# Five stream transposes in place of eight for the probabilities of the strided attention pieces

## The chip, the core and the metric

The kernel runs on one core of a Trainium2 chip. Its engines work side by side and wait for one another on semaphores: PE (TensorE, matrix products), DVE (VectorE), ACT (ScalarE), POOL (GpSimd) and SP (SyncE, which here only issues transfers). The metric is the device time of one launch in microseconds (us), as the median of three runs.

## The reference

Eight batches of eight heads, 576 positions of 64 features each. The first four heads see the last 32 positions, the last four heads ("strided") every 32nd position before their own. A gated layer of 512 to 1536 to 512 features follows.

```
mask_local = (rel >= 0) & (rel < 32)
mask_strided = (rel >= 0) & (pos[None, :] % 32 == pos[:, None] % 32)
scores = where(masks, 0.125 * q @ k.T, -1e9);  attn = softmax(scores)
x = (attn @ v) as 4608 x 512
out = (sigmoid(x @ w_gate) * (x @ w_val)) @ w_out
```

## The kernel before

Attention is done in pieces of two heads, four pieces to a batch, two local (even numbers) and two strided (odd numbers): 32 pieces in all. The pieces of batches 0 and 1 have names that begin with f, those of batches 2 to 7 are numbered 0 to 23. The four of batch 0 turn their probabilities on PE, and the change does not touch them. Of the 28 others, which turn theirs on DVE, 14 are strided.

Of one such piece the steps are: S, scores on PE (line 422); M, the mask added on DVE (L446); A and U, row maximum and subtraction on DVE (L462, L471); E, exponent on ACT (L486); N and W, row sum and scaling on DVE (L492, L502, L510); B, the turn on DVE; X, the weighing of the values on PE (L598 strided, L570 local), which reads the turned tile `pt`; H and R, the results copied away by ACT. Z, on POOL, sets the columns beyond the 54 keys (L380, L382), since a strided piece has 54 keys in rows of 64.

The turn of a strided piece (`turn_blocks`) has to transpose, within each half of the 128 partitions, a block of 64 x 64: queries lie on partitions, keys on columns, twelve such blocks one after another. A stream transpose turns squares of 32 x 32, so each of four bands of 32 partitions (`part`, 0 to 3) is turned in two instructions, one for each half of the columns, and each lands in its place in `pt`: eight instructions, `32x384`. For local pieces POOL first clears parts of `pt` (`clear`, step Y, L373), and eight other transposes (L534) follow. `pt`, `sb` (the probabilities) and `mx` have one buffer each.

The rest of the kernel is the gated layer. Batches 0 to 2 go through it straight: g and v (gate and value products, L677), o (L708). From batch 3 on pairs of batches go through a fast scheme with seven products in place of eight: sums of weights are built and stored (pa L892, pb L897, ph L902, pw L906, pd), groups of them loaded (r), half products G and V on PE (L980, tiles p and d), evictions c on ACT (L1002), ad, mu and sigmoids on DVE and ACT (L1007, L1024), differences ta to td (L1030), operands hx on ACT and hy on DVE or hyp on POOL (L1044, L1048), and output products Oa and Ob (L1059).

Every engine takes its instructions in the order of one list written out in the source, `ORDER`. A name that ends in p or v is the same step on the other of POOL and DVE (pa on POOL, pav on DVE). Pieces 1 to 23 of the list are spread between the products, so that PE has products while DVE works on a piece.

Of the kernel before, what the change touches and what calls it, by code (L numbers as in the profile page):

```python
# [96 lines left out]
x0.2 y0.2 wdp3.2 wu3.2 wl3.2 wlp2.2 wa4.2 o0.1 fg3.0 wd4.1 fg3.1 fQ1.2 wb4.2 s0.3 fg4.0 wdp5.0 wu5.0 ws4.2 wr7.1 m0.3 wu4.1 wl4.1 wl5.0 wb6.0 wb5.1
x0.3 y0.3 o0.2 wdp4.2 wu4.2 wa5.1 ws5.1 wd5.1 wu5.1 s0.4 fM1.1 wa6.0 wr5.2 wr6.1 wlp5.1 wa6.1 wb5.2 ws6.0 fg4.1 wlp4.2 wd6.0 wa5.2 wu6.0 wlp6.0 wr7.0
wb7.0 ws6.1 wr8.0 m0.4 wb6.1 x0.4 wd6.1 fg5.0 o0.3 wu6.1 ws5.2 wd5.2 wa7.0 pl2 ws7.0 fg5.1 wu5.2 wb6.2 wlp6.1 wa7.1 s0.5 fg6.0 wd7.0 ws7.1 wb7.1 wl5.2
wb8.0 wr8.1 wd7.1 wu7.1 wlp7.1 y0.4 m0.5 wu7.0 wl7.0 wa6.2 ws6.2 wd6.2 x0.5 y0.5 fg6.1 fA1.1 wr7.2 wa8.0 ws8.0 wb8.1 s0.6 wd8.0 wa8.1 m0.6 fg7.0 wr9.0  # L100
wb7.2 wu6.2 wl6.2 wa7.2 fU1.1 x0.6 wu8.0 ws7.2 wd7.2 ws8.1 fg7.1 s0.7 wl8.0 fg8.0 wu7.2 wl7.2 y0.6 wd8.1 o0.4 o0.5 m0.7 fE1.1 wr8.2 wa8.2 wb8.2 wr9.1
wa9.0 wb9.0 wr9.2 ws8.2 fN1.1 o0.6 ws9.0 x0.7 wd9.0 fWp1.1 fB1.1.2 fB1.1.3 wu8.1 fB1.1.1 wb9.1 wdp8.2 wu8.2 wlp8.1 fB1.1.0 wlp8.2 wa9.1 wr10.0 ws9.1
wd9.1 fg8.1 wb9.2 wu9.0 wl9.0 wa9.2 ws9.2 y0.7 wu9.1 s0.8 fS1.2 wa10.0 m0.8 wb10.0 wr10.1 wlp9.1 fM1.2 wdp9.2 x0.8 fg9.0 wa10.1 wu9.2 ws10.0 wdp10.0
wb10.1 wu10.0 s0.9 fV1.1 fX1.1 fA1.2 fU1.2 fE1.2 ws10.1 wd10.1 wlp9.2 wr10.2 wa10.2 fg9.1 wlp10.0 y0.8 wb10.2 ws10.2 fH1.1 wr11.0 wu10.1 fV1.2 wdp10.2
fn1.2 fN1.2 fQ1.3 fR1.1 fW1.2 fY1.2 wb11.0 o0.7 fL1.1 wa11.0 ws11.0 fg10.0 m0.9 s0.10 fS1.3 fB1.2.0 fB1.2.3 fB1.2.1 fB1.2.2 x0.9 wlp10.1 fg10.1 wr11.2
wdp11.0 wu11.0 o0.8 y0.9 wr11.1 fZ1.3 fM1.3 fA1.3 fX1.2 o0.9 fU1.3 wb11.1 wu10.2 wlp11.0 fg11.0 wlp10.2 wa11.1 ws11.1 fE1.3 wdp11.1 fH1.2 fR1.2 wu11.1
wlp11.1 m0.10 fg11.1 fN1.3 fW1.3 fV1.3 fL1.2 fB1.3.3 fB1.3.2 fB1.3.0 fB1.3.1 fX1.3 x0.10 wa11.2 ws11.2 s0.11 y0.10 m0.11 o0.10 fH1.3 fL1.3 fR1.3 g1.0
v1.0 x0.11 y0.11 wb11.2 wd11.2 wu11.2 wl11.2 oh0.11.0 s1.0 m1.0 LQ0 S0.0 M0.0 pl0 M0.1 LQ1 A0 D0 oh0.11.1 g1.1 x1.0 y1.0 U0 E0 po5 e0.0 e0.1 d0.1 Y0
# [1116 lines left out]
```

## Time and profile before

| | |
|---|---|
| median of three runs | 912.22 us (911.18 to 912.96) |
| profiled execution | 911.91 us |
| its span, first to last instruction | 910.1 us |
| PE, DVE, ACT, POOL busy | 894.6, 663.4, 470.5, 324.0 us |
| granted TensorE clock | 1.000 of full speed, all through |

The span is 1.8 us shorter than the execution's own time, which takes in what lies around it. Busy times of PE count pipelined products that overlap a little, so a wait of PE costs somewhat more than the idle time shown. The order of the instructions says where a step stands in an engine's queue; how long anything takes or waits is read from the trace.

### The profile page before, as it was taken

The numbers are of one execution on the slowest core, as the hardware profiler recorded it, in microseconds if no ns is written. First come the engines' busy times: TensorE is split into PE (matmuls) and PEld (weight loads), VectorE is DVE, ScalarE is ACT, GpSimd is POOL, SyncE is SP. The second block draws the span as 40 slices with busy tenths as digits, with TensorE's granted clock in tenths as the row PEclk, the third lists the DMA queues.
The fourth block names the chain that finished last, engine by engine and source line by source line (L and its number), as shares of the span: only waits on it lengthen the run. The fifth ranks groups of instructions, "written<-read, shape, count | busy, mean of one in ns | idle before, by whom it ended". The sixth has DMA issues, their size and how long they took to land.

```text
span 910.1 us, 17932 instructions
## 1 busy us (share of the span) xinstructions
PE 894.6 (98%) x7050; PEld 727.7 (80%) x7050; DVE 663.4 (73%) x1075; ACT 470.5 (52%) x864; POOL 324.0 (36%) x370
## 2 busy tenths in 40 slices
...
GB/s 347 328 251 136 205 116 195 207 259 242 131 207 117 154 97 226 273 268 291 256 243 252 219 240 245 215 172 206 236 169 226 185 219 197 206 200 208 219 217 131
DMA packets 116868, 193.62 MB, mean 213 GB/s; under 512 B 7600, under 2 KB 58800, under 8 KB 116784
## 3 DMA queue, kind: packets, MB, share of 16 engines
...
## 4 chain that ended last, share of the span: by engine, by line
PE 75%; DVE 17%; issue 3%; DMA 2%; ACT 2%; POOL 1%; SPq 0%; DVEq 0%; ACTq 0%
PE oc L1059 18%; PE p L980 16%; PE d L980 12%; PE o L708 8%; PE v L677 8%; PE g L677 8%; DVE pt L534 2%; DVE pt L544 2%; DVE mx L492 1%; DVE mx L462 1%; DVE sb L510 1%; DVE sb L471 1%; DVE hid L1007 1%; PE s L422 1%; DMA ring<-sets 1%
## 5 line engine op out<-in xcount | busy, mean ns | idle before, releaser
L980 PE MATMUL p<-xs,ring 128*128 128x512 f32 x864 | 209.9, 391 | 1.6 <-DVE hid L1021 0.8
L980 PEld LDWEIGHTS p<-xs,ring 128*128 128x128 f32 x864 | 161.2, 188 | 36.0 <-DVE hid L1021 0.9
L980 PE MATMUL d<-xs,ring 128*128 128x512 f32 x648 | 158.9, 390 | 0.4 <-DVE hid L1007 0.2
L980 PEld LDWEIGHTS d<-xs,ring 128*128 128x128 f32 x648 | 121.2, 188 | 26.5 <-DVE hid L1007 0.6
L1059 PE MATMUL oc<-hh,ring 128*128 128x512 f32 x312 | 104.5, 390 | 0.0
L708 PE MATMUL o<-w,hh 128*128 128x512 f32 x288 | 91.0, 397 | 0.0
L677 PE MATMUL v<-xh,w 128*128 128x512 f32 x256 | 85.3, 391 | 0.0
L677 PE MATMUL g<-xh,w 128*128 128x512 f32 x256 | 85.0, 391 | 0.2 <-ACT xh L634 0.2
L1007 DVE TENSOR_TENSOR e<-e,d 128x512 f32<-128x512 f32 x54 | 36.9, 683 | 64.9 <-PE d L980 47.0
L1059 PE MATMUL oc<-ops,ring 128*128 128x512 f32 x288 | 72.9, 389 | 0.0
L1044 ACT CAST hh<-hid 128x512 fp32r<-128x512 f32 x78 | 47.4, 621 | 47.6 <-PE oc L1059 35.7
L1030 POOL TENSOR_TENSOR hid<-hid,hid 128x512 f32<-128x512 f32 x19 | 27.8, 1466 | 115.7 <-DVE hid L1024 105.6
L1002 ACT COPY e<-p 128x512 f32<-128x512 f32 x54 | 31.7, 587 | 71.2 <-PE p L980 67.6
L1059 PEld LDWEIGHTS oc<-hh,ring 128*128 128x128 f32 x312 | 58.6, 188 | 12.1
L544 DVE STREAM_TRANSPOSE pt<-sb 32x384 f32<-32x384 f32 x112 | 63.8, 569 | 2.0
L1007 DVE TENSOR_TENSOR hid<-hid,d 128x512 f32<-128x512 f32 x54 | 36.8, 682 | 37.8 <-PE d L980 23.3
L1059 PEld LDWEIGHTS oc<-ops,ring 128*128 128x128 f32 x288 | 54.0, 188 | 11.3
L708 PEld LDWEIGHTS o<-w,hh 128*128 128x128 f32 x288 | 52.7, 188 | 11.4
L1059 PE MATMUL oc<-hl,ring 128*128 128x512 f32 x156 | 60.8, 390 | 0.1
L897 POOL TENSOR_TENSOR sum<-sum 128x128 f32<-128x128 f32 x96 | 52.0, 542 | 24.4 <-DVE sum L892 15.6
L1002 ACT COPY hid<-p 128x512 f32<-128x512 f32 x54 | 31.7, 586 | 49.3 <-PE p L980 49.1
L534 DVE STREAM_TRANSPOSE pt<-sb 32x320 f32<-32x320 f32 (+1 forms) x112 | 55.4, 494 | 2.4
...
## 6 DMA issues: line engine op xcount, KB each, us to landing
ring<-sets SPq DMA_DIRECT2D x126, 512.0 KB, 4.9
...
```

The lines of the kernel that those rows point to most:

```text
L422: nc.tensor.matmul(sc[j % len(sc)][g * m : (g + 1) * m, j // len(sc) * BANK + (s - lo) * kk : j // len(sc) * BANK + (s - lo + 1) * kk], q[ ...
L534: nc.vector.transpose(dst[band * LB : (band + 1) * LB, at : at + n, col * LB : (col + 1) * LB], src[part * LB : (part + 1) * LB, x : x + n ...
L544: nc.vector.transpose(dst[to : to + LB, :, col : col + LB], src[part * LB : (part + 1) * LB, :, h * LB : (h + 1) * LB])
L677: nc.tensor.matmul(o, w, x, start=first and n == 0, stop=last and n == len(todo) - 1)
L708: nc.tensor.matmul(acc[k][i], h[:, i * P : (i + 1) * P], w, start=f == 0 and n == 0, stop=f == NF - 1 and n == 2,)
L897: by.tensor_tensor(u[:, to], u[:, x], u[:, y], op=op)
L980: nc.tensor.matmul(to, w[:, (wi * 2 + c) * P : (wi * 2 + c + 1) * P], x[xi][:, c], start=p in (1, 2, 5) and c == j == 0, stop=c == 1 and j ...
L1002: nc.scalar.copy(x, two[m, 0])
L1007: nc.vector.tensor_tensor(x, x, two[m, 1], op=ALU.add)
L1030: by.tensor_tensor(h[to], h[x], h[y], op=ALU.subtract)
L1044: nc.scalar.copy(ops[q, p][0], hidden_tile(k, q, KEPT[str(p)]))
L1059: nc.tensor.matmul(chains[m, at], w[:, (wi * 2 + m) * P : (wi * 2 + m + 1) * P], x[xi], start=p in (1, 2, 5) and q == j == 0, stop=q == PA ...
```

## The change

`turn_blocks` now does the right halves of the columns of all 128 partitions in one instruction (part 0). Two of the four squares that this writes are in their place; two are not, and parts 1 and 2 write the lower left squares over them. Part 3 turns the two upper left squares. The square that is left out (queries 0 to 31, keys 32 to 53) is masked, since a query sees no later key; its place in `pt`, the left columns of the lower bands, is set to zero by POOL with the rest of the left columns before (`clear`, step Y, which strided pieces now have as well).

```diff
         def clear():
             pt = tiles["pt"] = pt_tile(f"pt{b}_{step}")
+            if not local:
+                nc.gpsimd.memset(pt[:, : 2 * ns * QB].rearrange("p (t k) -> p t k", k=QB)[:, :, :LB], 0.0)
+                return
             for n in (0, 2):
...
-            if "pt" not in tiles:
-                tiles["pt"] = attn_tile("pt", f"pt{b}_{step}")
             src, dst = (x[:, : 2 * ns * QB].rearrange("p (t k) -> p t k", k=QB) for x in (tiles["sb"], tiles["pt"]))
-            for h in range(2):
-                to, col = (part // 2 * 2 + h) * LB, part % 2 * LB
-                nc.vector.transpose(dst[to : to + LB, :, col : col + LB], src[part * LB : (part + 1) * LB, :, h * LB : (h + 1) * LB])
+            if part == 0:
+                nc.vector.transpose(dst[:, :, LB:], src[:, :, LB:])
+                return
+            for frm, to, col in (((1, 0, 1),), ((3, 2, 1),), ((0, 0, 0), (2, 2, 0)))[part - 1]:
+                nc.vector.transpose(
+                    dst[to * LB : (to + 1) * LB, :, col * LB : (col + 1) * LB], src[frm * LB : (frm + 1) * LB, :, :LB]
+                )
```

`ORDER` is written anew from its 187th step on. The steps are the same but for 14 clears (Y of the odd pieces, fY1.1, fY1.3) and some 80 steps that go from POOL to DVE or from DVE to POOL. One line of the list, with the weighing of piece 17:

```diff
-G3.4.1 c3.4.0.1 B17.2 pd4.2.0 r27 V3.4.1 c3.4.1.1 G3.4.2 G3.4.6 sg3.3.3 mu3.3.3 V3.4.6 V3.4.2 ad3.4.0.2 S18.1 pa5.2.0 R16 B17.0 B17.1 B17.3 X17.1
...
+S18.1 B17.2 B17.1 B17.3 pa5.2.0 R16 r27 G3.4.5 c3.4.1.6 ta3.3 ad3.4.1.2 H16 V3.4.5 M18.0 M18.1 A18 U18 E18 pb5.2.0 G3.4.7 r29 mu3.3.7 r30 mu3.4.2
+tc3.3 X17.1 Y18 LV18 N18 W18 c3.4.0.7 ad3.4.0.7 V3.4.7 c3.4.1.7 ad3.4.1.7 ph5.2.0.0 B18.0 LQ19 D18 G3.4.4 sg3.4.4 V3.4.4 r32 r31 B18.2 B18.1 B18.3 Z19
```

On DVE, at piece 15 (tiles `sb_3`, `pt_3`; `e`, `hid`, `d` and `p` are the gated layer's), the queue was before:

```order
L492 TENSOR_REDUCE mx_3_5062<-sb_3_5061 128x12
L502 RECIPROCAL mx_3_5062<-mx_3_5062 128x12
L510 TENSOR_TENSOR sb_3_5061<-sb_3_5061,mx_3_5062 128x12x54
L1007 TENSOR_TENSOR e_2_7_5153<-e_2_7_5153,d_2_4997 128x512
L544 STREAM_TRANSPOSE pt_3_5181<-sb_3_5061 32x12x32 x2
L1007 TENSOR_TENSOR hid_6_5115<-hid_6_5115,d_2_4972 128x512
L544 STREAM_TRANSPOSE pt_3_5181<-sb_3_5061 32x12x32 x6
```

and of the same piece on DVE it is now (line numbers are up to five higher):

```order
L495 TENSOR_REDUCE mx_3_5093<-sb_3_5092 128x12
L505 RECIPROCAL mx_3_5093<-mx_3_5093 128x12
L1012 TENSOR_TENSOR e_2_7_5124<-e_2_7_5124,d_2_4975 128x512
L513 TENSOR_TENSOR sb_3_5092<-sb_3_5092,mx_3_5093 128x12x54
L1012 TENSOR_TENSOR hid_6_5012<-hid_6_5012,d_2_4966 128x512
L1029 TENSOR_TENSOR hid_5_4973<-hid_5_4973,e_2_1_4964 128x512
L544 STREAM_TRANSPOSE pt_3_5148<-sb_3_5092 128x12x32
L547 STREAM_TRANSPOSE pt_3_5148<-sb_3_5092 32x12x32 x4
```

Eight transposes with an addition among them have become one of 128 partitions and four of 32, all behind the additions.

On POOL, from the padding of piece 15 on (`sum` and `sumh` are sums of weights), the queue was before:

```order
L380 MEMSET sb_3_5061 128x12
L382 MEMSET sb_3_5061 128x12x9
L906 TENSOR_TENSOR sum_2_0_4990<-sum_2_0_4990,sumh_2_0_5111 128x512
L897 TENSOR_TENSOR sum_2_1_5124<-sum_2_1_5124 128x128 x4
L1030 TENSOR_TENSOR hid_4_4901<-hid_3_4785,hid_2_4710 128x512
L906 TENSOR_TENSOR sum_2_1_5124<-sum_2_1_5124,sumh_2_1_5172 128x512
L1030 TENSOR_TENSOR hid_2_4710<-hid_4_4901 128x512
```

and on POOL it is now:

```order
L383 MEMSET sb_3_5092 128x12
L385 MEMSET sb_3_5092 128x12x9
L1035 TENSOR_TENSOR hid_4_4855<-hid_3_4751,hid_2_4713 128x512
L373 MEMSET pt_3_5148 128x12x32
L902 TENSOR_TENSOR sum_2_1_5106<-sum_2_1_5106 128x128 x4
L911 TENSOR_TENSOR sum_2_1_5106<-sum_2_1_5106,sumh_2_1_5206 128x512
L1035 TENSOR_TENSOR hid_3_4751<-hid_4_4855,hid_3_4751 128x512
```

The new clear of `pt_3` stands behind one subtraction of the gated layer and ahead of the sums of weights.

## Rows read from the trace of the kernel before

**Rows 1.** The page: span; busy us (share) and instructions of an engine.
```profile
span 910.1 us, 17932 instructions
...
PE 894.6 (98%) x7050; PEld 727.7 (80%) x7050; DVE 663.4 (73%) x1075; ACT 470.5 (52%) x864; POOL 324.0 (36%) x370
```

**Rows 2.** Stretches: length, PE, PEld, DVE, ACT, POOL busy; clock, DMA.
```profile
84.00:380.00 296.00, 292.76 (x2751) 238.23 (x2750) 242.16 (x437) 154.67 (x276) 121.84 (x168) 1.00 0.58 182
380.00:480.00 100.00, 95.91 (x1077) 77.20 (x1076) 94.95 (x156) 57.73 (x110) 53.85 (x75) 1.00 0.82 268
480.00:911.00 431.00, 426.13 (x2303) 350.57 (x2302) 258.12 (x370) 194.07 (x352) 111.27 (x87) 1.00 0.64 208
```

**Rows 3.** PE's waits, 84 to 380 us: releaser, us in total, times, longest.
```profile
PE x L598 <- PE v L677: 0.9, 1, 0.9
PE x_a L570 <- DVE pt L534: 0.7, 1, 0.7
PE s_v L422 <- DVE e L690: 0.5, 1, 0.5
```

**Rows 4.** PE's waits, 380 to 480 us, the five longest.
```profile
PE x L570 <- DVE pt L534: 1.1, 1, 1.1
PE x L598 <- DVE pt L544: 0.8, 2, 0.4
PE p L980 <- DVE hid L1021: 0.8, 1, 0.8
PE p L980 <- ACT e L1002: 0.5, 1, 0.5
PE p L980 <- ACT hid L1002: 0.3, 1, 0.3
```

**Rows 5.** PE in order of time: start, us, instructions, idle before.
```profile
118.61 0.99 PE L570 MATMUL x<-pt,vv 64*64 64x96 f32 x40
...
415.64 1.64 PE L570 MATMUL x<-pt,vv 64*64 64x96 f32 x40 [1.06 <-DVE pt L534]
```

**Rows 6.** DVE by shape: busy us, mean ns, idle before.
```profile
L544 DVE STREAM_TRANSPOSE pt<-sb 32x384 f32<-32x384 f32 x112 | 63.8, 569 | 2.0
L534 DVE STREAM_TRANSPOSE pt<-sb 32x320 f32<-32x320 f32 x84 | 42.2, 503 | 1.6
...
L446 DVE TENSOR_TENSOR sb<-s,cst 128x324 f32<-128x324 f32 x16 | 7.2, 488 | 0.0
```

**Rows 7.** POOL by shape: the clears and the padding.
```profile
L373 POOL MEMSET pt<- 128x320 f32 x28 | 9.3, 365 | 29.8 <-DVE hid L1030 20.8 <-DVE hl L701 5.2 <-PE x_a L598 3.7
L382 POOL MEMSET sb<- 128x108 f32 x16 | 3.2, 200 | 0.0
L380 POOL MEMSET sb<- 128x12 f32 x16 | 1.9, 119 | 66.0 <-DVE pt L534 66.0
```

**Rows 8.** The sums of weights by shape, on DVE and on POOL.
```profile
L897 DVE TENSOR_TENSOR sum<-sum 128x128 f32<-128x128 f32 x48 | 15.6, 326 | 1.4
L892 DVE TENSOR_TENSOR sum<-w 128x256 f32<-128x256 f32 x28 | 10.9, 434 | 3.7 <-DMA sets<-sum 3.7
...
L897 POOL TENSOR_TENSOR sum<-sum 128x128 f32<-128x128 f32 x96 | 52.0, 542 | 24.4 <-DVE sum L892 15.6 <-issue 1.5 <-POOL sb L382 0.6
L892 POOL TENSOR_TENSOR sum<-w 128x256 f32<-128x256 f32 x40 | 33.0, 843 | 51.9 <-DMA sets<-sum 22.3 <-DVE hl L701 15.9 <-DMA osets<-sum 11.9
```

**Rows 9.** DVE and POOL in order of time, near 408 and 436 us.
```profile
408.70 1.31 DVE L501 TENSOR_SCALAR mx<-mx 128x10 f32<-128x10 f32 x1
...
436.70 0.41 DVE L501 TENSOR_SCALAR mx<-mx 128x10 f32<-128x10 f32 x1
...
408.69 1.29 POOL L906 TENSOR_TENSOR sum<-sum,sumh 128x512 fp32r<-128x512 f32 x1
```

More of the change, by code (lines that the diff above doesn't have):

```diff
@@ L97 @@
[L97 to L108, printed above, removed]
@@ new lines @@
+wr10.1 wa10.1 wb10.1 s0.9 fX1.1 wu10.0 fA1.2 fU1.2 wlp9.2 fE1.2 ws10.1 wd10.1 wr10.2 wa10.2 fV1.2 fg9.1 wb10.2 y0.8 wlp10.0 ws10.2 wdp10.2 wr11.0
+wu10.1 fn1.2 fQ1.3 fN1.2 fW1.2 fH1.1 fR1.1 fg10.0 m0.9 o0.7 wa11.0 fL1.1 wb11.0 s0.10 fS1.3 wr11.1 ws11.0 fY1.2 fB1.2.0 fB1.2.3 wlp10.1 fg10.1 fB1.2.1
+fB1.2.2 wr11.2 wdp11.0 o0.8 x0.9 wu11.0 wlp11.0 wu10.2 fZ1.3 fM1.3 fA1.3 fU1.3 wb11.1 fX1.2 y0.9 m0.10 wa11.1 o0.9 fV1.3 fg11.0 fE1.3 wlp10.2 ws11.1
+wdp11.1 fH1.2 wu11.1 wlp11.1 fg11.1 fN1.3 fW1.3 fR1.2 fL1.2 fY1.3 fB1.3.0 fB1.3.1 s0.11 x0.10 fB1.3.2 fB1.3.3 wb11.2 y0.10 wa11.2 fX1.3 LQ0 o0.10
@@ new lines @@
+LV7 X7.0 ph5.0.0.1 pw5.0.0 pwp4.1.1 pd4.1.1 S8.0 LQ9 xl3.0.1 M8.0 M8.1 A8 U8 D8 oh2.3.1 pa5.0.1 pb5.0.1 Y8 pd5.0.0 E8 N8 W8 B8.2 o2.4 g2.6 R7 s2.6
+B8.0 pa5.1.0 pb5.1.0 B8.1 ph5.0.1.1 pwp5.0.1 v2.6 oh2.5.0 H7 B8.3 LV8 X8.0 Y9 m2.6 x2.6 S9.0 Z9 M9.0 M9.1 D9 oh2.5.1 g2.7 v2.7 ph5.1.0.0 pwp5.1.0 H8
+A9 U9 y2.6 E9 N9 W9 s2.7 g2.8 pd5.0.1 pa5.1.1 m2.7 pb5.1.1 pd5.1.0 xdv3.0.0 ph5.1.1.1 xh3.0.5 LQ10 LV9 xlp3.0.5 v2.8 B9.0 B9.1 B9.2 B9.3 pw5.1.1
+pd5.1.1 x2.7 y2.7 oh2.6.0 s2.8 m2.8 R8 X9.0 Y10 S10.0 M10.0 LQ11 M10.1 A10 U10 D10 oh2.6.1 H9 xd3.0.1 xdv3.0.2 xh3.0.6 v2.9 r1 LV10 E10 xh3.0.7
@@ new lines @@
+xl3.0.6 N10 x2.8 y2.8 W10 B10.0 B10.2 g2.9 B10.1 R9 xd3.0.3 o2.7 xh3.0.4 xlp3.0.4 xh3.1.2 xlp3.1.2 s2.9 B10.3 Z11 m2.9 x2.9 y2.9 oh2.8.0 X10.0 R10
+xh3.1.1 H10 xlp3.0.7 S11.0 M11.0 M11.1 D11 oh2.8.1 A11 U11 E11 N11 W11 xd3.1.0 xh3.1.5 Y11 xlp3.1.5 g2.10 s2.10 LQ12 B11.0 B11.2 r2 v2.10 m2.10 x2.10
+g2.11 y2.10 xl3.1.1 v2.11 oh2.9.0 po0 B11.1 B11.3 s2.11 m2.11 xh3.0.3 LV11 X11.0 pav0.2.0 pbv0.2.0 S12.0 M12.0 r4 H11 xd3.1.1 xh3.1.3 x2.11 M12.1 r3
+xh3.1.6 r0 A12 xlp3.1.6 y2.11 U12 LV12 xdv3.1.2 xh3.1.7 oh2.9.1 xdv3.1.3 o2.10 o2.11 e2.0 R11 xh3.1.4 G3.0.1 V3.0.1 e2.1 d2.0 xlp3.1.4 G3.0.2 E12
@@ new lines @@
+pa3.2.0 pb3.2.0 sg3.3.2 ph3.2.0.0 c3.3.0.6 ad3.3.1.2 c3.3.1.6 mu3.3.2 r22 V3.3.7 Y16 B16.2 LV16 R15 pw3.2.0 pd3.2.0 pa5.2.1 pb5.2.1 G3.3.7 S17.1
+ph5.2.1.1 B16.0 B16.1 V3.3.5 r24 pw5.2.1 r25 B16.3 X16.1 LV17 LQ18 c3.3.1.7 sg3.2.7 mu3.2.7 c3.3.0.7 G3.3.4 ad3.3.1.7 sg3.3.4 Z17 ad3.3.0.7 M17.0
+M17.1 D17 A17 U17 E17 tav3.2 hyp3.2.1 tcv3.2 V3.3.4 mu3.3.4 G3.3.3 ad3.3.0.3 sg3.3.7 pa4.2.0 pb4.2.0 hx3.3.1 ph4.2.0.0 V3.3.3 ad3.3.1.3 N17 r26
+hyp3.3.1 r28 pwp4.2.0 G3.4.1 c3.4.0.1 Y17 sg3.3.3 W17 B17.0 pd4.2.0 V3.4.1 c3.4.1.1 G3.4.2 ad3.4.0.2 G3.4.6 mu3.3.3 c3.4.0.6 V3.4.6 V3.4.2 sg3.4.2
@@ new lines @@
+N19 W19 Y19 B19.0 c3.5.0.6 V3.5.5 tb3.2 R18 r35 G3.5.7 xh5.0.1 c3.5.1.6 xlp5.0.1 V3.5.7 mu3.5.2 xh5.1.2 xlp5.1.2 c3.5.0.7 c3.5.1.7 xlp5.0.2 ad3.5.0.7
+sg3.5.7 ad3.5.1.7 pd5.2.0 mu3.5.7 r36 B19.2 G3.5.4 LQ20 V3.5.4 sg3.5.4 mu3.5.4 G3.5.3 ad3.5.0.3 r37 sg3.5.3 r38 B19.1 V3.5.3 r39 ad3.5.1.3 mu3.5.3
+tc3.4 Ob3.0.1 Ob3.1.1 Ob3.2.1 xdv5.0.0 Oa3.0.1 Oa3.1.1 hx3.0.2 B19.3 Ob3.3.1 ta3.5 hx3.5.1 hy3.5.1 Ob3.4.1 Oa3.2.1 tcv3.5 hx3.1.2 Oa3.3.1 hx3.2.2
+Oa3.4.1 hy3.0.2 hx3.3.2 tb3.5 Oa3.5.1 Ob3.5.1 ok3.1.1 hx3.4.2 pd5.2.1 r42 hy3.2.2 r40 hy3.1.2 xh5.0.3 td3.1 Oa3.0.2 Oa3.1.2 Oa3.2.2 tdv3.0 hy3.4.2
@@ new lines @@
+xl5.1.5 Oa3.0.5 hx3.4.5 hy3.4.5 Ob3.0.5 hx3.5.5 xdv5.1.1 Ob3.1.5 xh5.1.3 Oa3.1.5 hx3.0.7 hy3.0.7 Oa3.2.5 Oa3.3.5 xh5.1.6 hy3.5.5 Ob3.2.5 xdv5.1.2
+hx3.1.7 hy3.1.7 ok3.1.6 Oa3.4.5 Ob3.3.5 Ob3.4.5 hx3.2.7 xl5.1.6 hx3.3.7 xh5.1.7 hy3.3.7 Ob3.5.5 Oa3.5.5 ok3.0.6 LQ21 Ob3.0.7 Ob3.1.7 r48 hx3.4.7
+xl5.1.7 r49 Oa3.0.7 hx3.5.7 Oa3.1.7 r50 hx3.0.3 hy3.2.7 xdv5.1.3 xh5.1.4 Oa3.2.7 xlp5.1.4 ok3.1.5 Oa3.3.7 hy3.4.7 Oa3.4.7 hy3.5.7 td3.3 Ob3.2.7
+Ob3.3.7 Ob3.4.7 Ob3.5.7 U20 hy3.0.3 Oa3.5.7 Ob3.0.3 hx3.1.3 hy3.1.3 Ob3.1.3 hx3.2.3 hy3.2.3 hx3.3.3 ok3.0.5 Oa3.0.3 Oa3.1.3 Oa3.2.3 hx3.4.3 hy3.4.3
@@ new lines @@
+Ob5.4.1 hx5.3.2 Ob5.5.1 hx5.4.2 r94 Oa5.0.2 tcv5.5 xdv7.0.1 hy5.2.2 hyp5.4.2 xh7.0.6 tbv5.5 xh7.0.5 Oa5.1.2 Ob5.0.2 Ob5.1.2 r95 hx5.0.6 hy5.3.2
+ok5.1.1 Ob5.2.2 hx5.5.2 hy5.5.2 Oa5.2.2 Oa5.3.2 hyp5.0.6 Ob5.3.2 Ob5.4.2 ok5.0.1 hx5.2.6 hy5.2.6 r96 Oa5.4.2 Ob5.0.6 xl7.0.6 hx5.1.6 hyp5.1.6 hx5.3.6
+hy5.3.6 Ob5.5.2 xd7.0.3 Oa5.5.2 r97 oa5.1.2 tdv5.4 Oa5.0.6 hx5.4.6 hx5.5.6 hy5.5.6 Oa5.1.6 Ob5.1.6 hx5.0.5 hy5.0.5 hy5.4.6 r98 Ob5.2.6 tdv5.1 Oa5.2.6
+hx5.1.5 hy5.1.5 Ob5.3.6 Oa5.3.6 hx5.2.5 hyp5.2.5 xh7.0.4 Oa5.4.6 Oa5.5.6 Ob5.4.6 ok5.0.6 Ob5.5.6 hx5.4.5 oa5.0.2 Ob5.0.5 xl7.0.5 os5.1.2 xdv7.0.2
@@ new lines @@
+hx5.3.5 hy5.3.5 hy5.4.5 Oa5.0.5 hx5.5.5 Oa5.1.5 hy5.5.5 Oa5.2.5 Ob5.1.5 xh7.0.7 r99 xl7.0.7 Oa5.3.5 xdv7.1.0 xlp7.0.4 xdv7.1.1 hx5.0.7 Ob5.2.5 hx5.1.7
+hy5.1.7 Ob5.3.5 Oa5.4.5 hy5.0.7 Oa5.5.5 Ob5.4.5 Ob5.5.5 r102 ok5.1.6 r100 xh7.1.5 xl7.1.5 hx5.2.7 Oa5.0.7 Oa5.1.7 hy5.2.7 Oa5.2.7 xdv7.1.2 r101
+hx5.4.7 xh7.0.3 xh7.1.6 hx5.3.7 Ob5.0.7 tdv5.3 Ob5.1.7 xl7.1.6 hy5.4.7 xdv7.1.3 hx5.0.3 r103 hx5.5.7 hy5.5.7 hyp5.3.7 xh7.1.4 xh7.1.7 Ob5.2.7 hx5.1.3
+Ob5.3.7 Oa5.3.7 hx5.2.3 hy5.0.3 xl7.1.4 Ob5.4.7 Oa5.4.7 Ob5.5.7 ok5.0.5 hy5.1.3 xlp7.1.7 ok5.1.5 Oa5.5.7 oa5.0.7 Oa5.0.3 Oa5.1.3 hx5.3.3 Ob5.0.3
@@ new lines @@
+hx5.5.3 oa5.1.7 hyp5.2.3 Ob5.1.3 Ob5.2.3 Oa5.2.3 hy5.3.3 Oa5.3.3 hx5.4.3 hx5.0.4 hy5.4.3 Oa5.4.3 hx5.1.4 hy5.5.3 Ob5.3.3 tdv5.2 hx5.2.4 r104 hy5.0.4
+Oa5.0.4 hy5.1.4 os5.0.2 Oa5.1.4 Oa5.5.3 Ob5.4.3 hx5.3.4 hyp5.3.4 Ob5.5.3 r107 tdv5.5 hx5.4.4 r105 Ob5.0.4 hx5.5.4 hy5.2.4 hyp5.4.4 oa5.1.3 Oa5.2.4
+Ob5.1.4 Ob5.2.4 r106 Ob5.3.4 r108 hy5.5.4 Oa5.3.4 Oa5.4.4 Oa5.5.4 ok5.0.4 Ob5.4.4 Ob5.5.4 r109 ok5.1.4 oa5.0.3 G7.0.1 xlp7.0.3 c7.0.0.1 V7.0.1
+c7.0.1.1 r110 G7.0.2 G7.0.6 V7.0.2 ad7.0.0.2 sg7.0.2 ad7.0.1.2 V7.0.6 os5.1.7 r112 G7.0.5 mu7.0.2 hx7.0.1 c7.0.1.6 c7.0.0.6 V7.0.5 r113 G7.0.7
@@ new lines @@
+c7.2.1.6 V7.2.7 ad7.2.0.2 G7.2.5 c7.2.0.7 ad7.2.0.7 r121 G7.2.4 c7.2.1.7 tcv7.1 V7.2.4 r123 sg7.2.4 G7.3.1 sg7.2.2 mu7.2.2 tb7.0 G7.2.3 ad7.2.1.7
+V7.2.3 os5.1.3 r125 ad7.2.0.3 r124 G7.3.2 r126 c7.3.0.1 r127 hx7.2.1 mu7.2.4 ad7.3.0.2 ad7.2.1.3 sg7.2.3 mu7.2.3 sg7.2.7 mu7.2.7 V7.3.1 G7.3.6
+c7.3.0.6 hyp7.2.1 G7.3.5 c7.3.1.1 tav7.2 tbv7.2 G7.3.7 c7.3.0.7 V7.3.2 r128 V7.3.6 c7.3.1.6 r129 ad7.3.1.2 V7.3.5 V7.3.7 c7.3.1.7 ad7.3.1.7 G7.3.4
+sg7.3.4 r131 tc7.2 V7.3.4 ad7.3.0.7 G7.3.3 ad7.3.0.3 G7.4.1 mu7.3.4 sg7.3.7 mu7.3.7 V7.3.3 r130 r133 sg7.3.2 mu7.3.2 r132 sg7.3.3 G7.4.2 hy7.0.1
```

197 lines of the change are left out of this document (84 added, 113 removed).

## The prediction

> **What bounds the kernel now.** I read the page first: PE is busy for 894.6 of 910.1 us [rows 1], with the clock at full speed in every stretch [rows 2]. The change removes no product, so PE's own work stays, and only PE's idle time can go. The view by stretches says where that is. From 84 to 380 us PE lacks 296.00 - 292.76 = 3.2 us, from 380 to 480 us 4.1 us, and after 480 us, but for the end of the program, nearly nothing. The waits of the start-up, before 84 us, lie where the two lists still agree, and stay. Then DVE's column: 94.95 of 100 us are busy between 380 and 480 us, against 242 of 296 before that and 258 of 431 after [rows 2]. In those 100 us DVE is as full as PE; there the softmax of the pieces and the additions of the fast scheme meet. Last, PE's waits in both stretches: there turned tiles and sums that come from DVE, directly or by way of an ACT copy, make up 3.5 us in the five longest of the second stretch [rows 4] and 1.2 of the three longest of the first [rows 3]. So at PE's gaps DVE is mostly what is late, and work taken from DVE in front of them is worth something; elsewhere it is worth nothing.
>
> **The change part by part.** *Transposes.* A strided piece had eight of 0.569 us [rows 6]; now it has four of that shape and one of 128 partitions by 384 columns. The trace has no transpose of 128 partitions. Its cost from both sides: not under 0.488 us, which an addition on all 128 partitions takes for fewer columns, 324, and not over four times 0.569 = 2.28 us, if the four bands went one after another. Nearest is the comparison in [rows 6]: a transpose of 32 partitions by 320 takes 0.503 us and that addition takes 0.488 us, so a column costs the same however many partitions carry it. I take 0.569 us. Per piece 8 - 5 = 3 transposes go, 1.7 us; over 14 pieces 23.9 us (from 0 at the upper end to 25.0).
>
> The four small ones now wait for the large one, which writes two squares that they write over; they follow it on the same queue, and steps of a softmax that wait for each other there start without a visible gap, so I cost this at nothing (0.1 us a piece if not).
>
> *Clears.* 14 memsets of 128x384 on POOL. From 0.200 us for 108 columns and 0.365 for 320 [rows 7] a column costs 0.78 ns, so one takes 0.415 us and all 5.8 us. POOL is busy for 36% of the span [rows 1] and that is hidden. What is not hidden for certain is the wait: the clear cannot start before PE has weighed the piece before (`pt` has one buffer), POOL's queue stands still for that, and the first transpose cannot start before the clear. The local pieces have lived with the same pair of waits all along: DVE idled 1.6 us in all before the local transposes of the largest group [rows 6], 84 of them. In the queue of piece 15 one subtraction stands between padding and clear, and the sums of weights behind it. I take 0.1 us for each of 12 late pieces on DVE, 0 to 0.5.
>
> *Steps that change engine.* Ten fewer L892 and sixteen fewer L897 stand on DVE and as many more on POOL: DVE loses 10 x 0.434 + 16 x 0.326 = 9.6 us, POOL gains 10 x 0.843 + 16 x 0.542 = 17.1 us [rows 8]. Some other 128x512 steps go either way, seven to DVE and six from it; nearly even, I count them as nothing. So DVE goes from 663 to about 630 us, POOL from 324 to about 347.
>
> POOL's gain has a price on DVE: where both work on tiles of SBUF one can hold the other up. Of the same tiny L501 one took 1.31 us, started beside a POOL subtraction of 1.29 us, and one 0.41 us [rows 9]: 0.9 us for one meeting. If each added us of POOL's sums held DVE for a us, 17.1 of the 33.5 us would be given back; I take the meetings as now and then, and a fifth of it, 3.4 us, which leaves about 30 of the 33.5.
>
> The Trainium skill (SBUF — State Buffer, section "Who interferes with whom" and the list under "SBUF: two separate sides") has a rule on this that speaks against the moved sums: the port pair that DVE and GpSimd share is a lock for a whole instruction, and a DVE instruction takes it when it runs in a mode with both ports, or has two SBUF inputs while the GpSimd instruction reads SBUF; the loser waits in full. By that rule the clears, which read nothing, would cost DVE's additions nothing and the moved sums up to their length. The 1.31 us of L501 agrees with a whole instruction's wait.
>
> *What PE gets of it.* Between 380 and 480 us three strided pieces (13, 15, 17) are turned on DVE, 3 x 1.7 = 5.1 us less there, about as much as DVE's own idle time in the stretch, 5.05 us [rows 2], so DVE is no longer full. The five waits there sum to 3.5 us [rows 4]. A wait at a local weighing costs more than is shown, since the products start before the last band is turned: 1.64 us for 40 products against 0.99 us where nothing was late [rows 5], another 0.65. Of 4.2 us I take three quarters, 3.1: piece 17's weighing also moves behind three more half products in the list, which covers its 0.4 us. In the first stretch 1.2 us of [rows 3] hang on DVE; DVE is less full there and I take half, 0.6. Each wait that goes also gives back the refilling of PE's pipeline; with 8 such waits and 0.15 us each, which is an estimate (the idle time shown leaves out the overlap of two products), 1.2 us. Sum: 4.9 us gained. Against it I set 1.5 us of new waits, since a list written anew has its own gaps: as many as three at the mean of those in [rows 3, 4]. Net 3.4 us. On the profiled execution's 911.9 us that gives 908.5; the median stands 0.3 us above it, so 908.8 us.
>
> **The rivals.** *The relief is spent elsewhere (no change).* The places of scores and weighings among PE's products are nearly the same in both lists, so the same products stand between a piece's S and its X. If the chain S, M, A, U, E, N, W through DVE and ACT is what is late and not DVE's load, PE still waits at the same places, and 0.9 us of [rows 3] is a wait of PE on its own products which no transpose shortens. For it: ACT stands as releaser of 0.8 us in [rows 4]. Against it: DVE's 94.95 of 100. It would give 1 us or less, 911.3 to 912.5.
>
> *The large transpose takes its bands in turn, 2.28 us.* Then a turn costs what it did, only the 9.6 us of moved sums are gained, and as they are spread over 400 us PE gets about a tenth: 911.3 us. [Rows 6] speak against it.
>
> *POOL's lock on DVE.* Half the relief goes to meetings with the moved sums, as bounded above: PE's gain halves to 2.4 us before the 1.5 us of new waits, 911.3 us. The rule of the Trainium skill named above (SBUF — State Buffer, "Who interferes with whom") is the one that would do this. The 0.9 us of one meeting is for it, POOL's 53.85 of 100 us in the full stretch [rows 2] too, that the sums are only 17.1 us over the program against it.
>
> *The clear comes late (slower).* The padding of a strided piece holds POOL already: 66.0 us in eleven waits for DVE's transposes of the piece before [rows 7], 6 us each, and POOL's other work queues up behind it. The clear stands right after, behind one or more of those operations (1.3 us as L906 in [rows 9]; a group of four L897 2.2 us). If the transposes of the twelve late pieces each wait for one such group and half of that reaches PE, 12 x 2.2 / 2 = 13 us are lost against the 4.9 gained: about 920 us. With one L906 each it is 8 us, 915 us. It decides as soon as a clear ends 0.8 us after its piece's scaling (L510 before) in most pieces. Against it: the local clears hardly ever hold DVE up.
>
> *All waits go.* 7.3 us of idle, 1.3 of stretched weighings and 2 of refilling: 901.5 us at best; half way to it from my forecast is 905.
>
> **How the numbers follow.** Forecast (904.5 to 910.4): 0.64, in which 0.08 lies below 905.5. The three cases of little change, 0.13, 0.05 and 0.07; the late clear 0.09; 0.02 for what lies beside these. A measurement here tells 0.2% from no change, 1.8 us: faster means under 910.4, slower over 914.0. The forecast is faster; the little-change cases are the same; of the late clear a little would also end there. So 0.65 faster, 0.27 same, 0.08 slower. The range leaves out 0.08 below and about 0.12 above: 905.5 to 912.4.
>
> **What would show it.** Right: in the changed profile one transpose of 128x384 of about 0.57 us and 56 of 32x384; DVE near 630 us and visibly under 95 of 100 between 380 and 480 us; PE's idle time there down from 4.1 us to 2 or less, the waits on `pt` of L570 and L598 gone or halved. Wrong: DVE waiting before the large transpose for POOL's clear for more than 2 us in all; the large transpose over 1 us; or the same idle time of PE in that stretch under other names, with DVE's idle time grown by as much as its work fell.

## The result, and the profile after

The changed kernel took 901.73 us (median of four runs, 900.72 to 902.38), the kernel before 912.07 beside it: a ratio of 0.9886 [0.9869, 0.9903], 10.3 us less. I had forecast 3.4 us less, so the direction was right and the size was not.

The page of the changed kernel, which answers to [rows 1]: span, busy time of each engine, and the chain that ended last.

```profile
span 899.4 us, 17929 instructions
...
PE 890.6 (99%) x7050; PEld 725.9 (81%) x7050; DVE 630.3 (70%) x1008; ACT 475.0 (53%) x866; POOL 350.4 (39%) x409
...
PE 94%; DVE 4%; ACT 1%; issue 1%; POOL 0%; DVEq 0%; ACTq 0%; POOLq 0%
```

The same line of the kernel before:

```profile
PE 75%; DVE 17%; issue 3%; DMA 2%; ACT 2%; POOL 1%; SPq 0%; DVEq 0%; ACTq 0%
```

DVE has left the chain almost wholly. Of the 10.7 us that the span lost, 899.4 - 890.6 = 8.8 us of PE's idle time against 15.5 before make 6.7, and PE's own busy time fell by 4.0, though it does the same 7,050 products.

To see where, I compare stretches of equal work, each from one weighing to another. Of the kernel before (columns as in [rows 2]):

```profile
118.61:352.71 234.10, 231.11 (x2207) 187.86 (x2207) 188.12 (x346) 115.47 (x205) 93.74 (x139) 1.00 0.58 177
352.71:475.62 122.91, 119.64 (x1218) 96.85 (x1217) 111.75 (x191) 70.42 (x134) 59.55 (x84) 1.00 0.82 270
475.62:571.67 96.05, 95.16 (x657) 77.93 (x657) 76.66 (x110) 52.16 (x95) 35.32 (x30) 1.00 0.71 236
```

The same products in the changed kernel:

```profile
118.89:347.60 228.71, 228.71 (x2207) 186.70 (x2207) 173.32 (x304) 107.85 (x199) 109.02 (x165) 1.00 0.58 181
347.60:466.37 118.77, 118.51 (x1218) 96.09 (x1217) 106.84 (x179) 75.47 (x137) 66.52 (x92) 1.00 0.85 275
466.37:561.35 94.98, 94.98 (x658) 78.01 (x657) 74.57 (x109) 53.47 (x96) 33.43 (x27) 1.00 0.71 237
```

The first stretch gave 5.4 us, the second 4.1, the third 1.1: together 10.6. In the first, PE's idle time went from 234.10 - 231.11 = 2.99 us to nothing and its busy time fell by 2.40; in the second by 3.0 and 1.1. After 561 us next to nothing more is gained. All of PE's waits from 84 to 480 us, which answer to [rows 3, 4]:

```profile
PE s L425 <- DVE high L305: 0.8, 1, 0.8
PE x L575 <- POOL sb L383: 0.2, 1, 0.2
```

What DVE and POOL do for it, by shape, as in [rows 6 to 8]:

```profile
L537 DVE STREAM_TRANSPOSE pt<-sb 32x320 f32<-32x320 f32 x84 | 42.2, 502 | 1.5
L547 DVE STREAM_TRANSPOSE pt<-sb 32x384 f32<-32x384 f32 x56 | 31.8, 568 | 1.3
L544 DVE STREAM_TRANSPOSE pt<-sb 128x384 f32<-128x384 f32 x14 | 8.0, 573 | 0.5
L373 POOL MEMSET pt<- 128x384 f32 x14 | 5.9, 419 | 7.8 <-PE x L575 4.1 <-PE x_a L575 3.6
```

One transpose of 128 partitions costs what one of 32 does (573 and 568 ns), and DVE idled 0.5 us in all before the fourteen.

### The profile page after: what moved, and what is told of

The parts are those of the page before. It is cut to its first block, busy times and chain, and to the rows that moved or that the text cites. A ratio compares the mean times of both kernels' runs of the same rounds, so it can differ in the third digit from the quotient of the medians.

```text
span 899.4 us, 17929 instructions
## 1 busy us (share of the span) xinstructions
PE 890.6 (99%) x7050; PEld 725.9 (81%) x7050; DVE 630.3 (70%) x1008; ACT 475.0 (53%) x866; POOL 350.4 (39%) x409
## 4 chain that ended last, share of the span: by engine, by line
PE 94%; DVE 4%; ACT 1%; issue 1%; POOL 0%; DVEq 0%; ACTq 0%; POOLq 0%
PE p L985 21%; PE oc L1064 19%; PE d L985 15%; PE o L713 11%; PE v L682 10%; PE g L682 10%; PE s L425 1%; PE x L603 1%; PE s_g L425 1%; DVE pt L537 1%; PE x L575 1%; PE gv L682 1%; PE x_a L575 1%; PE x_a L603 1%; PE s_v L425 0%
## 5 line engine op out<-in xcount | busy, mean ns | idle before, releaser
L1053 POOL TENSOR_TENSOR hl<-hid,hh 128x512 fp32r<-128x512 f32 x23 | 31.9, 1385 | 115.2 <-ACT hh L1049 111.3
L1035 POOL TENSOR_TENSOR hid<-hid,hid 128x512 f32<-128x512 f32 x27 | 38.5, 1428 | 82.7 <-DVE hid L1029 56.1
L902 POOL TENSOR_TENSOR sum<-sum 128x128 f32<-128x128 f32 x112 | 62.2, 555 | 12.5 <-issue 2.3
L897 POOL TENSOR_TENSOR sum<-w 128x256 f32<-128x256 f32 x50 | 41.8, 855 | 56.9 <-DMA sets<-sum 19.5
L1053 DVE TENSOR_TENSOR hl<-hid,hh 128x512 fp32r<-128x512 f32 x55 | 44.4, 817 | 24.7 <-ACT hh L1049 24.6
```

The costliest lines, as they stand in the source:

```text
L897: by.tensor_tensor(to, part(wh[f][i], c), part(wl[f][i], c), op=ALU.add)
L902: by.tensor_tensor(u[:, to], u[:, x], u[:, y], op=op)
L1035: by.tensor_tensor(h[to], h[x], h[y], op=ALU.subtract)
L1053: by.tensor_tensor(hl, hidden_tile(k, q, KEPT[str(p)]), hh.bitcast(F32), op=ALU.subtract)
```

## The experiments

Every time is a median, with the kernel before measured beside it on the same chip. Runs e1 to e4 shared one chip (the kernel before took 911.53 us there), e5 to e8 a second (911.07) and e9 to e12 a third (911.34), so a difference between times of two groups, or with the 901.73 above, can be off by some tenths of a us, at most about 1. For where a variant lost or won I also numbered PE's 7,050 products and compared the start of the same number with the changed kernel; where the old list has a few products in another order this is off by some tenths. The table gives that delay in us, for the products that the changed kernel starts at the time on top, in the profiled run of each; those of e2, e5 and e11 lie 2 us above the medians of their variants, the others within 1.1 us.

| | 100 | 240 | 300 | 340 | 400 | 480 | 880 | DVE busy | time |
|---|---|---|---|---|---|---|---|---|---|
| before | 0.2 | 0.7 | 2.4 | 5.1 | 6.3 | 9.9 | 10.7 | 663.4 | 912.07 |
| e1_turn_only | 0.5 | -0.1 | 1.6 | 3.0 | 2.9 | 2.8 | 3.1 | 640.4 | 905.39 |
| e2_list_only | 2.0 | 2.9 | 4.5 | 6.9 | 7.4 | 10.8 | 12.2 | 656.3 | 911.26 |
| e3_turn_late_pieces | 0.5 | 1.1 | 2.8 | 5.2 | 5.2 | 5.2 | 6.2 | 657.1 | 907.65 |
| e7_turn_early_pieces | -0.3 | -0.9 | 0.9 | 3.0 | 4.5 | 8.6 | 8.9 | 651.4 | 909.50 |
| e4_engines_back | 0.0 | 0.9 | 3.1 | 8.5 | 8.6 | 8.7 | 9.1 | 641.8 | 911.28 |
| e11_sums_back | 1.6 | 2.5 | 4.4 | 9.3 | 9.5 | 10.5 | 10.5 | 638.2 | 909.78 |
| e12_rest_back | 0.0 | -0.1 | -0.2 | 0.8 | 0.9 | 1.1 | 1.5 | 634.2 | 903.63 |
| e5_load_before | 3.4 | 4.6 | 6.8 | 9.4 | 10.0 | 11.0 | 13.2 | 654.3 | 912.33 |
| e6_load_after | 0.9 | 1.5 | 3.3 | 5.2 | 5.6 | 8.0 | 9.3 | 651.7 | 911.13 |
| e9_load_one | 0.3 | 0.2 | 0.3 | 1.2 | 1.2 | 1.6 | 1.9 | 638.8 | 903.42 |
| e8_engines_only | 0.0 | 1.5 | 10.2 | 12.6 | 14.2 | 16.4 | 19.6 | 662.0 | 924.99 |

**The turn alone.** The code of the change under the old list; the clear stands right ahead of a piece's first transpose.

```diff
-B1.2
...
-B1.3 D1 B1.0 B1.1
+Y1 B1.0
...
+B1.1 D1 B1.2 B1.3
```

> The old list with the five transposes and the clear (put directly ahead of a piece's first transpose); no step changes engine. Load theory: DVE's work in front of the late weighings is what held PE, and 3 x 0.57 us of it go in every strided piece whatever the list: 902 to 905 us, PE's idle time from 84 us on under 2 us. List theory: the rewritten order closed the gaps, the transposes alone only shorten the few waits on a strided pt: 908 to 911 us.

Measured 905.39 us, 0.9937 [0.992, 0.9954]: 6.1 us less than the 911.53 beside it, just outside the load theory's range and far from the list theory's. From 340 us on it keeps pace with the changed kernel; the 3 us it lacks, it lost before. Two of its losses show where they come from. One is 1.1 us between 244 and 249 us. DVE of e1 there:

```profile
243.00 4.08 DVE L535 STREAM_TRANSPOSE pt<-sb 32x320 f32<-32x320 f32 x8
247.11 0.69 DVE L909 TENSOR_TENSOR sum<-sum,sumh 128x512 fp32r<-128x512 f32 x1
247.72 0.68 DVE L693 TENSOR_TENSOR e<-e,v 128x512 f32<-128x512 f32 x1
```

A sum of weights (pw) stands between the turn and the product `e`, and PE waits 0.52 us for `e` at 248.46. In the changed kernel that sum is on POOL and the product follows at once:

```profile
241.58 4.05 DVE L537 STREAM_TRANSPOSE pt<-sb 32x320 f32<-32x320 f32 x8
245.66 0.69 DVE L695 TENSOR_TENSOR e<-e,v 128x512 f32<-128x512 f32 x1
```

The other is 0.6 us at 276 us. There four sums (pb) stand between the halves of a local piece's turn, which ends at 276.43; DVE and PE of e1:

```profile
273.11 1.27 DVE L900 TENSOR_TENSOR sum<-sum 128x128 f32<-128x128 f32 x4
...
276.68 0.96 PE L573 MATMUL x_a<-pt,vv 64*64 64x96 f32 x39 [0.53 <-POOL sb L381]
```

In the changed kernel the turn of that piece runs in one go, its eight transposes take 4.08 us from 269.84, and the weighing at 275.06 has no wait.

**The list alone.** The new list with the old eight transposes and no clear.

```diff
             if not local:
-                nc.gpsimd.memset(pt[:, : 2 * ns * QB].rearrange("p (t k) -> p t k", k=QB)[:, :, :LB], 0.0)
                 return
...
-            if part == 0:
-                nc.vector.transpose(dst[:, :, LB:], src[:, :, LB:])
-                return
+            for h in range(2):
```

> The new list with the old eight transposes and no clear of strided pieces. Load theory: the new list is laid out for a DVE that has 24 us less, so PE waits again for turned tiles: 907 to 912 us. List theory: 902 to 905 us, since order is what closed the gaps.

Measured 911.26 us, 0.9996 [0.9984, 1.0007]: nothing. With the turn the same list was worth 905.39 - 901.73 = 3.7 us more than the old one (4.2 by what each gained on the kernel before beside it, so about 4), and the parts do not add.

**The turn in pieces 13, 15 and 17 alone, and in the earlier ones alone** (old list).

```diff
+        five = not local and b >= 2 and 4 * (b - 2) + step in (13, 15, 17)
```
```diff
+        five = not local and not (b >= 2 and 4 * (b - 2) + step >= 13)
```

> The old list, the five transposes and the clear only in the strided pieces 13, 15 and 17, whose turns lie between 380 and 480 us; 5.1 us less DVE work, all in the stretch where DVE was 95% busy. Load theory: PE gets back what it lost there, 4 to 5 us, and nothing before: 907 to 908.5 us, with the waits of 84 to 380 us unchanged. If DVE's being full there was not the limit, under 1.5 us: 910.5 to 912 us.

> The old list, with the five transposes in the strided pieces up to piece 11 and those of batch 1, and eight in 13 to 23: the counterpart of the run with pieces 13, 15 and 17. If the gains of the stretches add up (6.1 us with all pieces, 3.9 with the late three): 2 us less than before, 909 to 910 us. If a piece's relief is lost again at a later wait: 911 to 912 us.

Measured 907.65 us, 0.996 [0.9945, 0.9975], and 909.50 us, 0.9979 [0.9962, 0.9996]: 3.9 and 1.6 us less, together 5.5 of the 6.1 (pieces 19, 21 and 23 have eight transposes in both). Both lie where they were expected if the load counts and its gains add up. The table shows each gain where its pieces are. From 340 to 480 us the kernel before loses 4.8 us on the changed one, e3 nothing, e7 5.6; before 340 us e3 loses as much as the kernel before, e7 only 3.0.

**DVE's load put back**, three further small transposes per strided piece, ahead of the large one or behind the last one (the second writes what nobody reads).

```diff
             if part == 0:
+                for _ in range(3):
+                    nc.vector.transpose(dst[:LB, :, LB:], src[LB : 2 * LB, :, :LB])
```
```diff
+            for _ in range(3 * int(part == 3)):
+                nc.vector.transpose(src[:LB, :, :LB], src[LB : 2 * LB, :, :LB])
```

> The changed kernel with three more small transposes ahead of the large one in every strided piece (they write a square that is written over afterwards): DVE's load is back at 654 us, and the extra 1.7 us lie in front of the weighing. Load theory and place theory alike: PE waits for the turned tile again as with the new list and eight transposes (911.3 us): 909 to 912 us.

> The same three transposes, but right behind the last one of the piece, into the tile of the probabilities, which nothing reads any more: DVE has the same 654 us, the piece's own weighing doesn't wait for them. Load theory (DVE's busy time decides): 909 to 912 us, as with the extra ones in front. Place theory (only work in front of what PE waits for next decides): 902 to 906 us.

Measured 912.33 us, 1.0011 [0.9997, 1.0025], a little over what was expected, and 911.13 us, 0.9997 [0.9988, 1.0007]. 21 to 24 us more on DVE (the table) take back the whole 10 us wherever they stand in a piece, so it is DVE's work that counts, and not only how late the piece's own `pt` is. With the load behind the turn, the longest of PE's waits from 84 to 480 us are mostly on other tiles:

```profile
PE s L425 <- DVE xl L645: 1.1, 1, 1.1
PE x L577 <- POOL sb L383: 1.1, 1, 1.1
PE p L987 <- DVE hid L1028: 1.0, 1, 1.0
PE x_a L605 <- ACT xr L654: 1.0, 1, 1.0
```

The second is a local weighing whose turn ended 0.25 us before it began, at 415.81, so it waits for a turned tile although POOL's padding is named.

**A third of that load**, one further small transpose.

```diff
             if part == 0:
+                nc.vector.transpose(dst[:LB, :, LB:], src[LB : 2 * LB, :, :LB])
```

> The changed kernel with one more small transpose ahead of the large one in every strided piece: 8 us more on DVE, a third of the run with three (which gave 912.3 us). If DVE has no slack left in the new list, a third of that loss: 904.5 to 906 us. If the new list has some slack, as the changed kernel's last waits of 0.8 us suggest: 901.5 to 903 us.

Measured 903.42 us, 0.9912 [0.9894, 0.9931], between the two ranges: 1.7 us for 8 us of DVE, 0.2 per us; the next 13 to 16 us (e6, e5) cost 7.7 and 8.9, 0.6 per us. The new list has a little room on DVE, and past that more than half of what is added reaches PE.

**The clear three times.**

```diff
             if not local:
+                nc.gpsimd.memset(pt[:, : 2 * ns * QB].rearrange("p (t k) -> p t k", k=QB)[:, :, :LB], 0.0)
+                nc.gpsimd.memset(pt[:, : 2 * ns * QB].rearrange("p (t k) -> p t k", k=QB)[:, :, :LB], 0.0)
```

> The changed kernel with the clear of strided pieces done three times on POOL: 0.84 us later for the first transpose of every strided piece if the clear is what it waits for, 12 us more on POOL. If the clear is hidden, as DVE's 0.5 us of idle time before all 14 large transposes says: 901 to 902.5 us. If the clear is in the way: 904 us or more.

Measured 901.73 us, 0.9895 [0.9876, 0.9913], as without. DVE by shape, with the idle time ahead last:

```profile
L546 DVE STREAM_TRANSPOSE pt<-sb 128x384 f32<-128x384 f32 x14 | 8.0, 572 | 0.5
```

The clear has more than 0.8 us to spare before it holds DVE up.

**The 84 steps back on their old engines**, in the new list with the turn: all of them, then the 26 that are sums of weights (pa, pb, pw), then the 58 others.

```diff
-pbv0.0.1
+pb0.0.1
...
-pa0.1.1
+pav0.1.1
...
-xl3.0.1
+xlp3.0.1
```

> The changed kernel in its new order, but each of the 84 steps that changed between POOL and DVE is put back on the engine it had; DVE has 9.6 us more of sums of weights, POOL less. If the moved sums carry part of the gain (DVE relief of any kind counts): 903 to 905 us. If only the relief in the turn counts, since it lies in front of the weighing: 901.5 to 902.5 us.

> The changed kernel in its new order, with only the 26 sums of weights (pa, pb, pw) put back on the engine they had. With all 84 steps put back the gain was gone (911.3 us). If DVE's load is what counts, the sums are the part that matters (DVE 7 us more): 908 to 911 us.

> The counterpart: only the 58 other steps (operands and differences of the gated layer) put back on the engine they had; DVE's load changes by about 2 us. If DVE's load is what counts: 902 to 904 us. If the order fits only the engines that it was written for: 906 us or more.

Measured 911.28 us, 0.9998 [0.9988, 1.0007]; 909.78 us, 0.9983 [0.9971, 0.9995]; 903.63 us, 0.9917 [0.9896, 0.9938]: 9.6, 8.0 and 1.9 us lost against 901.73. The first is a miss for both branches of what was expected. The sums lose more than their load: e11's DVE is as busy as e9's, 638.2 and 638.8 us, but it loses 8.0 us and not 1.7. The table puts its largest loss, 4.8 us, between 300 and 340 us. PE there in e11, in order of time:

```profile
310.11 0.38 PE L573 MATMUL x_a<-pt,vv 64*64 64x96 f32 x4 [2.18 <-DVE pt L535]
311.23 1.20 PE L573 MATMUL x_a<-pt,vv 64*64 64x64 f32 x32 [0.74 <-DVE pt L535]
```

DVE and POOL of e11 just before:

```profile
306.13 0.98 DVE L535 STREAM_TRANSPOSE pt<-sb 32x288 f32<-32x288 f32 x2 [1.53 <-POOL pt L374]
307.53 1.27 DVE L900 TENSOR_TENSOR sum<-sum 128x128 f32<-128x128 f32 x4 [0.42 <-POOL sum L895]
308.81 1.01 DVE L535 STREAM_TRANSPOSE pt<-sb 32x320 f32<-32x320 f32 x2
...
301.43 0.74 POOL L895 TENSOR_TENSOR sum<-w 128x256 f32<-128x256 f32 x1 [2.73 <-DMA sets<-sum]
...
302.94 2.55 POOL L900 TENSOR_TENSOR sum<-sum 128x128 f32<-128x128 f32 x4
305.43 0.67 POOL L374 MEMSET pt<- 128x320 f32 x2
```

and the same turn in the changed kernel, in one go:

```profile
299.49 4.09 DVE L537 STREAM_TRANSPOSE pt<-sb 32x320 f32<-32x320 f32 x8
```

Read upward: a sum on POOL waits for a transfer, the clear of a local piece stands behind it, DVE's transposes wait 1.53 us for the clear, more sums stand among the transposes, and PE stands for 2.18 and 0.74 us. This is the late clear of my rival, but in a local piece, and only with the sums on the wrong engine. The two stops sum to 2.92 us; the rest of the loss there goes with the slower weighing and the lower clock behind the stops, which the last section shows.

**The new engines under the old list**, with the old turn.

```diff
-pb0.0.1
+pbv0.0.1
...
-pav0.1.1
+pa0.1.1
```

> The old list and the old turn, but the 84 steps that changed engine stand on the engine that they have now: DVE has 9.6 us less of sums of weights, POOL 17 us more. Load theory: some of that relief returns to PE, 908 to 911 us. Place theory: the sums lie between pieces and mostly not in front of a weighing, and POOL's later sums hold others up: 911 to 914 us.

Measured 924.99 us, 1.0143 [1.0125, 1.0161]: 13.9 us slower, a miss for every theory. ACT, POOL and PE of it, in order of time:

```profile
256.30 0.62 ACT L900 CAST sumh<-sum 128x512 fp32r<-128x512 f32 x1 [6.99 <-POOL sum L895]
...
252.82 1.42 POOL L890 TENSOR_TENSOR sum<-w 128x256 f32<-128x256 f32 x2 [3.38 <-DMA sets<-sum]
254.19 2.08 POOL L895 TENSOR_TENSOR sum<-sum 128x128 f32<-128x128 f32 x4
...
262.05 0.80 PE L675 MATMUL g<-xh,w 128*128 128x512 f32 x1 [5.21 <-ACT e L683]
```

A sum moved to POOL waited for a transfer, ACT's rounding of it stood 6.99 us at the head of ACT's queue, and the sigmoid `e` that PE needed stood behind it in that queue: PE stood for 5.21 us. That is about 7 of the 14 us (the table, 240 to 300 us, less the kernel before's own 1.7). Four more come at the end, after 875 us, where PE waits for operands of the last products that were moved with the rest:

```profile
PE oc L1057 <- DVE hl L1046: 2.1, 1, 2.1
PE oc L1057 <- DVE ops L1046: 1.4, 1, 1.4
```

The remaining 3 us come in small steps that I did not follow. DVE's busy time shows one more thing: at the means of the kernel before, the 84 steps that moved would take 8.1 us from DVE (9.6 by L892 and L897, some back by the others) and leave 655.3 us, but it came to 662.0.

## Why the prediction was wrong in size

**What bounds the kernel: right.** DVE was late at PE's gaps, and the work taken off it came back as time (e1; e5 and e6 take it away again). "Elsewhere it is worth nothing" was too strict for the first stretch, as below.

**Transposes, clears, moved sums: right.** The large transpose took 0.573 us for 0.569 forecast, the clear 0.419 for 0.415, DVE came to 630.3 us for about 630 and POOL to 350.4 for 347. The clear is hidden (e10).

**POOL's price on DVE: 3.4 us too many.** DVE's total came out as the bare sum of the removed work. By shape some instructions of DVE got cheaper and some dearer. The largest group that adds two SBUF tiles got cheaper; in the changed kernel:

```profile
L1029 DVE TENSOR_TENSOR hid<-hid,e 128x512 f32<-128x512 f32 x54 | 41.9, 783 | 23.2 <-ACT e L1020 22.0
```

and before:

```profile
L1024 DVE TENSOR_TENSOR hid<-hid,e 128x512 f32<-128x512 f32 x54 | 43.2, 808 | 13.5 <-ACT e L1015 12.2
```

The Trainium skill (SBUF — State Buffer, "Who interferes with whom") says that such an addition is held up by a GpSimd instruction that reads SBUF. That single meetings cost time is in [rows 9]; that 17 us more of GpSimd's sums cost DVE nothing in sum is in DVE's total, 630.3 us for a bare 629.9. It is not so under every list: with the same steps moved, DVE came out 1.0 us dearer than its means before would make it in e2 (656.3 us for 655.3), and 6.7 us dearer in e8 (662.0). So the price depended on what stands beside what, which I had no row for; that meetings with POOL are the whole of the 6.7 is not shown.

**What PE gets of it: this step failed.** Between 380 and 480 us I took three quarters of 4.2 us and most of the refilling, about 4; the equal stretch gave 4.1 and e3 shows that the three turns alone do it. Before 380 us I took half of 1.2 us, 0.6, and the stretch up to 353 us gave 5.4. Of these the turn alone gave 2.1 (before and e1 at 340 us in the table, 5.1 and 3.0), and the list the other 3, which I had at nothing. After 480 us I counted on nothing and 0.8 came. Three things were wrong with the 0.6.

First, I read DVE's 82% as room. A mean over 300 us says little about the few us ahead of a weighing. In the 6 us ahead of the one at 128.86 us DVE, the third busy time of the row, works for 5.86 us:

```profile
122.86:128.86 6.00, 5.13 (x23) 3.95 (x22) 5.86 (x12) 3.14 (x5) 1.58 (x1) 1.00 1.00 334
```

Second, I took the releasers at their word. Before, on DVE and then on PE:

```profile
124.11 4.65 DVE L544 STREAM_TRANSPOSE pt<-sb 32x384 f32<-32x384 f32 x8
...
128.86 0.91 PE L598 MATMUL x<-pt,vv 54*64 54x54 f32 x44 [0.88 <-PE v L677]
```

The wait is put down to PE's own product, and I set it aside as one that no transpose shortens [rows 3]. But the eight transposes ended at 128.76, 0.1 us before the weighing began. In the changed kernel the same weighing has no wait:

```profile
128.19 0.91 PE L603 MATMUL x<-pt,vv 54*64 54x54 f32 x44
```

A fourth wait of the first stretch, as long as the third of [rows 3], I left out altogether:

```profile
PE x_a L570 <- POOL sb L380: 0.5, 1, 0.5
```

It is put down to POOL's padding, but it too is a weighing right behind a turn, which ended at 277.25, 0.26 us before it began; e1 keeps it, as shown there.

Third, a late turn costs PE more than the idle time shown, because the weighing starts on the first bands and then crawls, and because every stop leaves out the overlap of two products. I counted the crawling for one weighing, 0.65 us [rows 5]. It was in more. One from the first stretch, before:

```profile
303.95 0.39 PE L677 MATMUL v<-xl,w 128*128 128x512 f32 x1
304.17 0.39 PE L677 MATMUL v<-xh,w 128*128 128x512 f32 x1
305.26 1.64 PE L570 MATMUL x_a<-pt,vv 64*64 64x96 f32 x40 [0.70 <-DVE pt L534]
```

and after, as fast as the undisturbed one of [rows 5]:

```profile
303.43 1.00 PE L575 MATMUL x_a<-pt,vv 64*64 64x96 f32 x40
```

Over the program this group of 168 went from 6.9 to 5.3 us. The refilling of the pipeline that I added as an estimate is in the same rows: the two products start 0.22 us apart and last 0.39, the weighing starts 1.09 us after the second, and only 0.70 of that is shown as idle, so the stop cost 0.16 us more than its idle time. I had 8 such waits in mind; from 84 to 480 us the kernel before has 16 stops of over 0.05 us and the changed one 3. By the starts of the products between 84 and 480 us, idle time shown fell by 6.2 us, refilling by 2.6 (I had 1.2) and the rest, which holds the crawling, by 0.9.

**New waits: 1.5 us against it, hardly any came.** From 84 to 480 us 1.0 us of waits is left in all. (Three at the mean of [rows 3, 4], nine waits of 5.6 us together, would have been 1.9 and not 1.5.)

**The list: a term put at nothing.** I gave it no gain. It is worth about 4 us, but only with the turn (e2) and its own engines (e4, e11), and the table shows where: between 240 and 340 us, where e1 falls back by 3. The two places shown under e1, 1.1 and 0.6 us, are of one kind: a sum of weights on DVE ahead of what PE waits for next. I had spread the 9.6 us of moved sums over 400 us and set them at about a tenth. So of the 6.9 us by which the forecast was short, about 1.5 are the turn before 380 us, 1.5 the new waits, and some 4 the list.

**The rivals.** "The relief is spent elsewhere" and "the bands in turn" fall with e1 and the 573 ns. "POOL's lock" falls with DVE's total in the changed kernel; e8's total leaves room for it under another list. "The clear comes late" does not happen in the strided pieces (0.5 us before fourteen transposes), though e11 shows that its mechanism exists. "All waits go" is what happened: its 901.5 us is 0.2 from the result, and 0.08 was too little for it. Its terms were 7.3 us of idle, 1.3 of stretched weighings and 2 of refilling; 6.2, 0.9 and 2.6 came. Before 84 us PE still waits; what went is what stands behind.

**Left open:** 3 of the 14 us of e8, and the share of the list's 4 us that other places than the two shown have. The profiled runs of e2, e5 and e11 lost 1.6 to 3.4 us before 100 us, mostly in the start-up, where the experiments change nothing. In e5 and e11 the granted clock from 20 to 30 us was 0.67 and 0.83, against 1.00 in the changed kernel; in e2 it was 1.00, and PE waited 1.0 us for a transfer. These are the runs that lie 2 us above their medians, and no conclusion rests on that part.
